# Agent attention and a gated convolution: three of five shifted operand rows copied by VectorE instead of by DMA

## The chip, the cores and the metric

The kernel runs on one core of a Trainium2 chip. The time is what the device takes for one execution, in microseconds (us). Before the change the median of three runs is 430.09 us (429.39 to 432.08). The core has TensorE (PE in the profile, with PEld for its weight loads), VectorE (DVE), ScalarE (ACT), GpSimd (POOL), and SyncE (SP), whose queue issues nearly all DMAs of this kernel; 16 DMA engines move the data.

## The reference

The inputs are q, k and v of 4 batches, 12800 rows and 128 channels, 49 "agent" rows per batch, and three weight arrays. Agents attend to the keys; the queries attend to the agents; the result passes a causal convolution of 5 taps per channel as a sigmoid gate, beside a linear projection, and a second projection.

```python
a2k = sm(agents, k)             # softmax(scale * agents @ k^T): 49 x 12800
agent_v = a2k @ v               # 49 x 128
q2a = sm(q, agents)             # 12800 x 49
x = q2a @ agent_v               # 12800 x 128
gate_pre = sum(conv_w[k] * shifted(x, 4 - k) for k in range(5))
out = (sigmoid(gate_pre) * (x @ w_val)) @ w_out
```

## The kernel before

Rows run along the free dimension. The kernel never forms x. What the gate and the value need is linear in the 49 query weights q2a, so per batch the convolution's taps, `w_val` and `agent_v` are folded into small weight tiles (`fold_weights`, line 110): tile `stat` holds eight 128x128 f16 blocks, five for the taps, one for the value, and two "rest" blocks that carry what f16 rounding leaves.

**Query weights as matmul operand.** A unit is 1280 rows, 10 units to a batch, 40 in all. For a unit (`queries`, line 667) TensorE makes scores, VectorE transposes them in 32x32 blocks, takes the maximum, and with GpSimd (subtract) and ScalarE (exp) forms the softmax `qw`. Tile `pt` then gets, per row, 128 f16 columns: 49 rounded weights (ScalarE, line 713), 49 rounding rests (GpSimd, line 726), and the first 30 rounded weights once more (GpSimd, line 718), so that they can meet the rest of the weights' own rounding. `transposes` (line 734) turns `pt` into 1280 columns of `x1`: for units 0 to 3 by TensorE with two copies (ScalarE line 764, VectorE line 769), for the other 36 by a DMA transpose that SP issues (line 743).

**The second operand x2.** The other 19 agents do not fit into the 128 rows of `x1`. `shifts` (line 774) copies rows 29 to 48 of `x1` (20 rows; `X2LO`, `X2R`) to five places of `x2`, one for each tap, each shifted by one more column, by five DMAs (line 791): once for each of the units 0 to 3 and then once for each pair of units, 18 pairs. `x2` has three buffers of 2560 columns.

**Chunks.** The output is made in chunks of 512 rows, 100 of them, the last in two halves. For a chunk TensorE runs five gate matmuls (line 828), one with `x2` (line 832), one for the value (line 855) and one with `x2` for it (line 859). ScalarE makes tanh `th` (line 841), VectorE the product `h` (line 868), ScalarE its f16 part `hh` (line 874), GpSimd the rest `hl` (line 879). Two chunks later TensorE projects with three matmuls (lines 898 to 900), ScalarE scales into `ob` (line 912) and SP stores it. The gate and the value have one PSUM bank each: TensorE can start the value of the next chunk only when `h` has read this one's.

**Order.** Every step is entered in a `Plan` with its engine, a cost in us and what it reads and writes. TensorE's steps keep the order in which they are entered (a list that weaves scores, agent values, the fold and the chunks together). The other engines' and SP's steps are put in order by a list scheduler (`Plan.order`, line 89) that goes by the entered costs and the length of the chain behind a step; a DMA is taken to land after its bytes and 1.4 us (`LAND`), and no more than 8 are in flight (`LANES`). What comes out is a fixed order on each engine; at run time each engine takes its instructions strictly in that order and waits where an operand is late.

Of the kernel before, what the change touches and what calls it, by code (L numbers as in the profile page):

```python
# [9 lines left out]
F32 = mybir.dt.float32  # L10
# [4 lines left out]
AX = mybir.AxisListType  # L15
# [16 lines left out]
X2LO = 29  # L32
X2R = 20
# [18 lines left out]
T_AT = 7  # L52
HOP = 0.09
# [9 lines left out]
class Plan:  # L63
# [7 lines left out]
    def __init__(self):  # L71
        self.steps, self.urge = [], []
        self.wrote, self.read = {}, {}

    def add(self, engine, us, fn, reads=(), writes=(), moved=0.0, key=None, urge=0.0):
# [11 lines left out]
        self.urge.append(urge)  # L87

    def order(self):
# [32 lines left out]
        while done < n:  # L122
# [49 lines left out]
def tile_agent_attention_gated_conv(  # L172
# [11 lines left out]
    A = 49  # L184
    NU = N // UNIT
# [12 lines left out]
    def ring(n, shape, dtype, name, pool=const):  # L198
        return [pool.tile(shape, dtype, name=f"{name}{i}") for i in range(n)]
# [12 lines left out]
    qw = ring(3, [P, NBLK, A], F32, "qw")  # L212
# [52 lines left out]
    for t in wst_sb:  # L265
        nc.gpsimd.memset(t[:, TAPS + 1 :, :], 0.0)

# [6 lines left out]
    def weights():  # L274
# [4 lines left out]
        else:  # L279
# [51 lines left out]
            for fn in ops:  # L331
# [5 lines left out]
                out=cmax, in_=conv_sb, axis=AX.X, op=ALU.max, apply_absolute_value=True  # L337
# [41 lines left out]
    def key_scores(b, u):  # L379
# [13 lines left out]
        if not first:  # L393
# [5 lines left out]
                out=kmx[b % 2][:, u, :], in_=src, axis=AX.X, op=ALU.max  # L399
# [6 lines left out]
    def key_max(b):  # L406
# [6 lines left out]
                out=m2, in_=kmx[x].rearrange("p u j -> p j u"), axis=AX.X, op=ALU.max  # L413
# [9 lines left out]
        def spread():  # L423
            nc.vector.tensor_reduce(
                out=mrow, in_=p1[0:2, 0:P].rearrange("j (g a) -> j a g", g=G),
                axis=AX.X, op=ALU.max,
# [58 lines left out]
    def fold_weights(b):  # L485
# [19 lines left out]
        def normalise():  # L505
            dve.tensor_scalar_add(den, pt[:, 0:A], 1e-9)
            dve.reciprocal(out=den, in_=den)
            dve.tensor_tensor(out=avT, in0=pt[:, AP_ : AP_ + A], in1=den, op=ALU.mult)

# [10 lines left out]
        def gate_scale():  # L520
            dve.tensor_reduce(
                out=mx[:, 0:1], in_=avT, axis=AX.X, op=ALU.max, apply_absolute_value=True
# [18 lines left out]
        x2g = wst[:, TAPS + 1, 0 : TAPS * X2R].rearrange("p (k r) -> p k r", k=TAPS)  # L541
        x2v = wst[:, TAPS + 2, 0 : TAPS * X2R].rearrange("p (k r) -> p k r", k=TAPS)
        ghi = wst[:, 0:TAPS, 0:A]
        vhi = wst[:, TAPS, 0:A]
        off = NDUP - X2LO

# [6 lines left out]
        def val_weights():  # L553
            dve.tensor_reduce(
                out=mx[:, 1:2], in_=pv[:, 0:A], axis=AX.X, op=ALU.max,
# [8 lines left out]
            rest(wst[:, TAPS, 2 * A :], pv[:, 0:NDUP], 1, vhi[:, 0:NDUP])  # L564
            rest(x2v[:, HALO, off:], pv[:, NDUP:A], 1, vhi[:, NDUP:])
# [10 lines left out]
        add("dve", 1.2, val_weights, [at_v], [(*w_, "v"), "mxv"])  # L576
        add(
            "act", 0.4,
            lambda: nc.scalar.copy(out=wst[:, 0:TAPS, A : 2 * A], in_=ghi),
# [3 lines left out]
            "act", 0.22, lambda: nc.scalar.copy(out=wst[:, TAPS, A : 2 * A], in_=vhi),  # L583
            [(*w_, "v")], [(*w_, "e")],
        )
        add("dve", 0.7, gate_rest, ["gw", (*w_, "g")], [(*w_, "r")])
# [46 lines left out]
        def split():  # L633
            dve.tensor_reduce(
                out=oscale, in_=po[:, 0:P], axis=AX.X, op=ALU.max, apply_absolute_value=True
# [31 lines left out]
    def queries(b, u):  # L667
# [6 lines left out]
        sa = sT[:, :, 0:A]  # L674
# [4 lines left out]
            lambda: nc.vector.tensor_reduce(out=qmx[x], in_=sa, axis=AX.X, op=ALU.max),  # L679
# [5 lines left out]
                out=d, in0=sa, in1=qmx[x].unsqueeze(2).to_broadcast([P, NBLK, A]),  # L685
# [10 lines left out]
        def sums():  # L696
            nc.vector.tensor_reduce(out=sm, in_=e, axis=AX.X, op=ALU.add)
# [9 lines left out]
                out=w, in0=e, in1=r.unsqueeze(2).to_broadcast([P, NBLK, A]), op=ALU.mult  # L707
# [5 lines left out]
            "act", 0.58, lambda: nc.scalar.copy(out=pt[:, :, 0:A], in_=w),  # L713
# [5 lines left out]
                out=pt[:, :, 2 * A :], in0=w[:, :, 0:NDUP], scalar1=1.0, scalar2=0.0,  # L719
# [7 lines left out]
                out=pt[:, :, A : 2 * A], in0=w, in1=pt[:, :, 0:A], op=ALU.subtract  # L727
# [7 lines left out]
    def transposes(b, u):  # L735
# [3 lines left out]
        if not on_pe(b, u):  # L739
# [7 lines left out]
                [(*p_, n) for n in range(3)], [("x1", u)], 2.4,  # L747
# [26 lines left out]
    def shifts(b, u):  # L774
# [9 lines left out]
        src = [(x, v) for v in range(max(u0 - 1, 0), u + 1) for x in ("x1", "x1b")]  # L784
        for k in range(TAPS):
            c = PAD - HALO + u0 * UNIT + k

            q, e = (nc.scalar, "act") if g == 0 and k % 2 else (nc.sync, "dma")
            add(
                e, 0.75,  # L790
                lambda k=k, c=c, q=q: q.dma_start(
                    out=x2[k * X2R : (k + 1) * X2R, o : o + n * UNIT],
                    in_=x1[X2LO : X2LO + X2R, c : c + n * UNIT],
                ),
                src, [("x2", s % 3, o + i * UNIT, k) for i in range(n)], 0.26 * n,
            )
# [6 lines left out]
    def gates(t):  # L803
# [17 lines left out]
        x2k = [("x2", segs_[0] % 3, h, k) for h in halves for k in range(TAPS)]  # L821
# [3 lines left out]
        def matmuls():  # L825
            for k in range(TAPS):
# [6 lines left out]
                out=pg, lhsT=stat[0 : TAPS * X2R, TAPS + 1, :],  # L833
                rhs=x2[0 : TAPS * X2R, o2 : o2 + w], start=False, stop=True,
# [13 lines left out]
    def values(t):  # L848
# [5 lines left out]
        def matmuls():  # L854
# [5 lines left out]
                out=pv, lhsT=stat[0 : TAPS * X2R, TAPS + 2, :],  # L860
                rhs=x2[0 : TAPS * X2R, o2 : o2 + w], start=False, stop=True,
# [196 lines left out]
```

## Time and profile before

| | |
|---|---|
| median of 3 runs | 430.09 us |
| the profiled execution's own time | 431.22 us |
| its span in the profile | 429.4 us |
| mean granted TensorE clock | 0.996 |
| busy: PE, DVE, ACT, POOL | 402.9, 297.0, 300.4, 224.3 us |
| DMA: bytes moved, mean rate | 128.07 MB, 298 GB/s |

The span is the time from the first to the last instruction, and 1.8 us of the execution's time lie outside of it. In the rows that follow, "x5" is a count of instructions; in a row of waits stand the total, the number and the longest; in a timeline stand start, length, engine, line, and in brackets the idle time of the engine just before, with what ended it.

### The profile page before, as it was taken

Reading aid. Unit: us, or ns where it says so; the run is one execution under the profiler, and the core shown is the slowest. Engines: PE = TensorE matmul, PEld = TensorE weight load, DVE = VectorE, ACT = ScalarE, POOL = GpSimd, SP = SyncE. Lnnn points to the kernel's source line nnn. Section 1 sums busy time; section 2 is a strip of 40 time slices with the busy share of each in tenths; the row PEclk is TensorE's granted clock in tenths of the full one; section 3 lists DMA queues with packets and bytes.
Section 4 is the critical chain, followed back from the end, with each engine's and each line's share of the span. In section 5 each row is a group of like instructions: output and inputs, shape, how many; then the busy total and the mean of one; then the engine's idle time right before and its main releaser. Section 6 shows DMA issues by size and latency. Waiting matters only on the chain.

```text
span 429.4 us, 8968 instructions
## 1 busy us (share of the span) xinstructions
PE 402.9 (94%) x3307; PEld 194.8 (45%) x3307; DVE 297.0 (69%) x555; ACT 300.4 (70%) x520; POOL 224.3 (52%) x239
## 2 busy tenths in 40 slices
PE   3978888999999999999999999999999999999995
PEld 1357333345565444444555544445555544434443
DVE  3776879886786877578666887678666787566231
ACT  1464536678976577778876676778876577777875
POOL 1002246564466665544557665553356466687553
PEclk9999989999999999999999999999999999999999
DMA  8999999999999999999999999999999999887743
GB/s 288 422 415 415 371 350 337 297 285 309 343 358 294 249 270 289 307 309 305 340 329 356 292 323 292 320 312 334 306 330 257 289 291 287 215 199 173 192 156 122
DMA packets 76158, 128.07 MB, mean 298 GB/s; under 512 B 51644, under 2 KB 51900, under 8 KB 76116
## 3 DMA queue, kind: packets, MB, share of 16 engines
q1 hardware_dynamic: 76056, 127.41, 96.0%
q8 instruction: 26, 0.43, 0.4%
q14 instruction: 16, 0.13, 0.1%
q10 hardware_dynamic: 60, 0.10, 0.1%
HBM read 79.25 MB, written 26.21 MB: 246 GB/s over the span
## 4 chain that ended last, share of the span: by engine, by line
PE 65%; DMA 13%; DVE 12%; ACT 5%; issue 3%; SPq 1%; POOL 1%; DVEq 0%; ACTq 0%; POOLq 0%
PE gate L828 20%; PE sc L363 13%; PE av L463 6%; PE gate L832 4%; PE val L855 4%; PE val L859 4%; PE out L898 4%; PE out L899 4%; PE out L900 4%; DMA ld<-qT 3%; DMA ld<-vP 3%; DVE h L868 2%; ACT e L455 2%; DMA ld<-kT 2%; DMA outT<-ob 2%
## 5 line engine op out<-in xcount | busy, mean ns | idle before, releaser
L879 POOL TENSOR_TENSOR hl<-h,hh 128x512 f16<-128x512 f32 (+1 forms) x101 | 117.0, 1160 | 121.3 <-ACT hh L874 113.7
L828 PE MATMUL gate<-x,stat 128*128 128x512 f16 (+1 forms) x500 | 124.4, 378 | 2.4 <-ACT th L841 2.3
L868 DVE SCALAR_TENSOR_TENSOR h<-th,val 128x512 f32<-128x512 f32 x100 | 67.7, 677 | 69.1 <-PE out L899 46.1
L363 PE MATMUL sc<-ld,ag_sb 128*32 128x320 f32 x1280 | 102.0, 452 | 10.0 <-DMA ld<-kT 8.0
L912 ACT ACTIVATE ob<-out,oscale 128x512 f32<-128x512 f32 x98 | 67.2, 686 | 23.5 <-PE out L900 17.4
L841 ACT ACTIVATE th<-gate,unscale 128x512 f32<-128x512 f32 x100 | 68.3, 683 | 19.7 <-PE gate L832 18.0
L828 PEld LDWEIGHTS <-stat 128*128 128x128 f16 x505 | 45.6, 97 | 66.4 <-issue 19.0
L874 ACT CAST hh<-h 128x512 f16<-128x512 f32 (+1 forms) x101 | 61.4, 608 | 13.1 <-DVE h L868 12.4
L684 POOL TENSOR_TENSOR qw<-sT,qmx 128x490 f32<-128x490 f32 x40 | 41.5, 1038 | 50.2 <-DVE qmx L679 50.1
L363 PEld LDWEIGHTS sc<-ld,ag_sb 128*32 128x32 f32 x1280 | 37.0, 112 | 62.8 <-issue 22.5
L463 PE MATMUL av<-ld,eT 128*64 128x129 f32 x800 | 49.5, 275 | 1.7 <-DMA ld<-vP 1.4
L389 ACT COPY ks<-sc 128x640 f32<-128x640 f32 x40 | 27.7, 691 | 32.7 <-PE sc L363 30.6
L463 PEld LDWEIGHTS av<-ld,eT 128*64 128x64 f32 x800 | 43.7, 136 | 11.7 <-issue 7.3
L726 POOL TENSOR_TENSOR pt<-qw,pt 128x490 f16<-128x490 f32 x40 | 44.7, 1119 | 3.8 <-ACT pt L713 3.1
L455 ACT ACTIVATE e<-ks,kbias 128x320 f32<-128x320 f32 x80 | 39.0, 553 | 6.1 <-DVE kbias L444 3.3
L373 DVE STREAM_TRANSPOSE eT<-e 128x640 f32<-128x640 f32 x40 | 33.6, 842 | 11.4 <-ACT e L455 5.9
L373 DVE STREAM_TRANSPOSE sT<-sc 128x640 f32<-128x640 f32 x40 | 33.3, 834 | 10.8 <-PE sc L363 10.6
L398 DVE TENSOR_REDUCE kmx<-ks 128x2 f32<-128x640 f32 x39 | 31.4, 817 | 11.8 <-ACT ks L389 11.8
L832 PE MATMUL gate<-x,stat 100*128 100x512 f16 x100 | 38.0, 380 | 0.8 <-DMA x<-x 0.8
L855 PE MATMUL val<-x,stat 128*128 128x512 f16 x100 | 37.8, 378 | 0.1
L859 PE MATMUL val<-x,stat 100*128 100x512 f16 x100 | 37.8, 378 | 0.0
L898 PE MATMUL out<-hh,wo 128*128 128x512 f16 x98 | 37.1, 379 | 0.0
(125 smaller groups left out, 392.1 us busy)
## 6 DMA issues: line engine op xcount, KB each, us to landing
ld<-vP SPq DMA_DIRECT2D x40, 645.0 KB
ld<-kT SPq DMA_DIRECT2D x40, 640.0 KB
ld<-qT SPq DMA_DIRECT2D x40, 640.0 KB
outT<-ob SPq DMA_DIRECT2D x48, 512.0 KB
x<-x SPq DMA_DIRECT2D x90, 100.0 KB
x<-x SPq DMA_DIRECT2D x18, 50.0 KB
outT<-ob SPq DMA_DIRECT2D x3, 256.0 KB
x<-pt SPq DMA_TRANSPOSE x36
```

The costliest lines, as they stand in the source:

```text
L363: nc.tensor.matmul(out=out[g * BLK : (g + 1) * BLK, j, 0:GT], lhsT=ag_sb[:, b, j * BLK : (j + 1) * BLK], rhs=src[:, g * GT : (g + 1) * GT] ...
L373: nc.vector.transpose(out=out.rearrange("p n (j i) -> p j n i", j=2), in_=in_.rearrange("p j (n i) -> p j n i", i=BLK),)
L463: nc.tensor.matmul(out=av[o : o + AP_, 0 : C + 1], lhsT=et[:, n, :], rhs=vt[:, n, :], start=(u == 0 and n < 2), stop=(u == NU - 1 and n >= ...
L828: nc.tensor.matmul(out=pg, lhsT=stat[:, k, :], rhs=x1[:, c : c + w], start=(k == 0), stop=False,)
L832: nc.tensor.matmul(out=pg, lhsT=stat[0 : TAPS * X2R, TAPS + 1, :], rhs=x2[0 : TAPS * X2R, o2 : o2 + w], start=False, stop=True,)
L841: lambda: nc.scalar.activation(out=th, in_=pg, func=AF.Tanh, scale=unscale[:, 0:1]),
L855: nc.tensor.matmul(out=pv, lhsT=stat[:, TAPS, :], rhs=x1[:, PAD + n0 : PAD + n0 + w], start=True, stop=False,)
L859: nc.tensor.matmul(out=pv, lhsT=stat[0 : TAPS * X2R, TAPS + 2, :], rhs=x2[0 : TAPS * X2R, o2 : o2 + w], start=False, stop=True,)
L868: lambda: nc.vector.scalar_tensor_tensor(out=h, in0=th, scalar=1.0, in1=pv, op0=ALU.add, op1=ALU.mult),
L874: "act", 0.16 + 0.42 * scale, lambda: nc.scalar.copy(out=hh, in_=h),
L879: lambda: nc.gpsimd.tensor_tensor(out=hl, in0=h, in1=hh, op=ALU.subtract),
L912: lambda: nc.scalar.activation(out=ob[:, o : o + w], in_=po, func=AF.Copy, scale=oscale),
```

## The change

**Rows of x1.** The rows of `x1` (the columns of `pt`) now begin with two agents in duplicate: rows 0 and 1 are agents 28 and 29 once more, rows 2 to 50 the 49 rounded weights, 51 to 99 the rests, 100 to 127 agents 0 to 27 again. The host puts the two extra agents ahead of the others in the agents' array, so scores, subtraction, exp and product run over 51 columns instead of 49; the sum leaves the two out, and the duplicate copy of line 718 is 28 columns wide instead of 30. By this the 19 agents that go to `x2` stand in rows 32 to 50, the beginning of a quarter of the 128 partitions.

**x2.** Its 128 rows are now used as five blocks by tap: taps 0, 2 and 4 at rows 0, 32 and 64, tap 1 at row 97, tap 3 in two pieces at rows 116 and 20. Taps 0, 2 and 4 are copied by VectorE (19 rows, 1280 or 2560 columns), taps 1 and 3 by three DMAs of 20, 12 and 8 rows; of an odd number of rows one more is moved, which meets a weight of zero. The two matmuls with `x2` read 128 rows instead of 100, and GpSimd zeroes the three `x2` buffers once at the start. In the fold the rest weights now go to more places: nine short VectorE instructions instead of four. The planner is told that a DMA transpose lands 2 us later than before for those who wait for it (`SPARE`).

```diff
+A0 = 2
+HI0, LO0, DUP0 = A0, 51, 100
+REST = 32
+X2_ROWS = (
+    ((0, 19, 0),),
+    ((0, 19, 97),),
+    ((0, 19, 32),),
+    ((0, 12, 116), (12, 7, 20)),
+    ((0, 19, 64),),
+)
+SPARE = 2
...
-                end = max(wire, when + us) + LAND
-                lanes = lanes[1:] + [end]
+                end = max(wire, when + us) + LAND + self.spare[i]
+                lanes = lanes[1:] + [end - self.spare[i]]
...
+    for t in x2s:
+        nc.gpsimd.memset(t, 0.0)
...
-            rest(wst[:, TAPS, 2 * A :], pv[:, 0:NDUP], 1, vhi[:, 0:NDUP])
-            rest(x2v[:, HALO, off:], pv[:, NDUP:A], 1, vhi[:, NDUP:])
+            rest(wst[:, TAPS, DUP0:], pv[:, 0 : P - DUP0], 1, vhi[:, 0 : P - DUP0])
+            rest(wst[:, TAPS, 0:A0], pv[:, P - DUP0 : NDUP], 1, vhi[:, P - DUP0 : NDUP])
+            for i, n, r in X2_ROWS[HALO]:
+                i += NDUP
+                rest(wst[:, TAPS + 2, r : r + n], pv[:, i : i + n], 1, vhi[:, i : i + n])
...
-            rest(wst[:, 0:TAPS, 2 * A :], gw[:, :, 0:NDUP], 0, ghi[:, :, 0:NDUP])
-            rest(x2g[:, :, off:], gw[:, :, NDUP:], 0, ghi[:, :, NDUP:])
+            n = P - DUP0
+            rest(wst[:, 0:TAPS, DUP0:], gw[:, :, 0:n], 0, ghi[:, :, 0:n])
+            rest(wst[:, 0:TAPS, 0:A0], gw[:, :, n:NDUP], 0, ghi[:, :, n:NDUP])
+            quads = wst[:, TAPS + 1, 0 : 3 * REST].rearrange("p (k r) -> p k r", k=3)
+            rest(quads[:, :, 0:NREST], gw[:, 0:TAPS:2, NDUP:], 0, ghi[:, 0:TAPS:2, NDUP:])
+            for k in range(1, TAPS, 2):
+                for i, n, r in X2_ROWS[k]:
+                    i += NDUP
+                    rest(
+                        wst[:, TAPS + 1, r : r + n], gw[:, k, i : i + n], 0,
+                        ghi[:, k, i : i + n],
+                    )
...
         for k in range(TAPS):
             c = PAD - HALO + u0 * UNIT + k
...
-            add(
-                e, 0.75,
-                lambda k=k, c=c, q=q: q.dma_start(
-                    out=x2[k * X2R : (k + 1) * X2R, o : o + n * UNIT],
-                    in_=x1[X2LO : X2LO + X2R, c : c + n * UNIT],
-                ),
-                src, [("x2", s % 3, o + i * UNIT, k) for i in range(n)], 0.26 * n,
-            )
+            for i, m, r in X2_ROWS[k]:
+                out, in_ = x2[r : r + m, o : o + w], x1[REST + i : REST + i + m, c : c + w]
+                keys = [("x2", s % 3, o + j * UNIT, k, i) for j in range(n)]
+                if k % 2 == 0:
+                    add(
+                        "dve", 0.08 + 0.33 * n,
+                        lambda out=out, in_=in_: nc.vector.tensor_copy(out=out, in_=in_),
+                        src, keys,
+                    )
+                    continue
...
+                add(
+                    e, 0.75, lambda out=out, in_=in_, q=q: q.dma_start(out=out, in_=in_),
+                    src, keys, 0.013 * m * n,
+                )
...
-                out=pg, lhsT=stat[0 : TAPS * X2R, TAPS + 1, :],
-                rhs=x2[0 : TAPS * X2R, o2 : o2 + w], start=False, stop=True,
+                out=pg, lhsT=stat[:, TAPS + 1, :], rhs=x2[:, o2 : o2 + w],
+                start=False, stop=True,
```

TensorE's order stays as it was. On the other engines much is moved; three places follow. The first is VectorE in the fold of the first batch, between the rounded value weights and `unscale`; `wst0` is the tile of folded weights, `val` and `gw` what they are made of, `rs` their scale. Before:

```order
L548 SCALAR_TENSOR_TENSOR wst0_118<-val_131,rs_162,wst0_118 128x30
L548 SCALAR_TENSOR_TENSOR wst0_118<-val_131,rs_162,wst0_118 128x19
L548 SCALAR_TENSOR_TENSOR wst0_118<-gw_161,rs_162,wst0_118 128x5x30
L548 SCALAR_TENSOR_TENSOR wst0_118<-gw_161,rs_162,wst0_118 128x5x19
L613 TENSOR_SCALAR unscale0_124<-mx_160 128x2
```

The same place now:

```order
L561 SCALAR_TENSOR_TENSOR wst0_118<-val_131,rs_165,wst0_118 128x28
L561 SCALAR_TENSOR_TENSOR wst0_118<-val_131,rs_165,wst0_118 128x2
L561 SCALAR_TENSOR_TENSOR wst0_118<-val_131,rs_165,wst0_118 128x19
L561 SCALAR_TENSOR_TENSOR wst0_118<-gw_164,rs_165,wst0_118 128x5x28
L561 SCALAR_TENSOR_TENSOR wst0_118<-gw_164,rs_165,wst0_118 128x5x2
L561 SCALAR_TENSOR_TENSOR wst0_118<-gw_164,rs_165,wst0_118 128x3x19
L561 SCALAR_TENSOR_TENSOR wst0_118<-gw_164,rs_165,wst0_118 128x19
L561 SCALAR_TENSOR_TENSOR wst0_118<-gw_164,rs_165,wst0_118 128x12
L561 SCALAR_TENSOR_TENSOR wst0_118<-gw_164,rs_165,wst0_118 128x7
L639 TENSOR_SCALAR unscale0_124<-mx_163 128x2
```

Four instructions became nine over the same 294 elements per partition; nothing else moved between them.

The second place is VectorE in the third batch, around the product `h0` of chunk 60 (chunks are counted from 0); `eT` and `sT` are block transposes of key and query scores, `qmx` a maximum. Before:

```order
L868 SCALAR_TENSOR_TENSOR h2_108<-th2_105,val_131 128x512
L373 STREAM_TRANSPOSE sT1_86<-sc0_128 128x2x10x32
L679 TENSOR_REDUCE qmx1_88<-sT1_86 128x10
L373 STREAM_TRANSPOSE eT2_84<-e0_80 128x2x10x32
L373 STREAM_TRANSPOSE eT0_82<-e1_81 128x2x10x32
L373 STREAM_TRANSPOSE eT1_83<-e0_80 128x2x10x32
L868 SCALAR_TENSOR_TENSOR h0_106<-th0_103,val_131 128x512
```

The same place now, where `x21` is the buffer of `x2` for units 26 and 27:

```order
L910 SCALAR_TENSOR_TENSOR h2_108<-th2_105,val_131 128x512
L389 STREAM_TRANSPOSE sT1_86<-sc0_128 128x2x10x32
L821 COPY x21_101<-x1_99 19x2560
L389 STREAM_TRANSPOSE eT2_84<-e0_80 128x2x10x32
L389 STREAM_TRANSPOSE eT0_82<-e1_81 128x2x10x32
L910 SCALAR_TENSOR_TENSOR h0_106<-th0_103,val_131 128x512
L821 COPY x21_101<-x1_99 19x2560 x2
L910 SCALAR_TENSOR_TENSOR h1_107<-th1_104,val_131 128x512
```

One copy now stands ahead of two transposes and the `h` of chunk 60, and two more ahead of the `h` of chunk 61; the maximum `qmx1` and one transpose went behind.

The third place is SP for the same pair of units: `pt0` is unit 27, whose transpose completes the pair. Before:

```order
L927 DMA outT<-ob1_116 128x1024
L743 DMA_TRANSPOSE x1_99<-pt0_96 128x10x128
L358 DMA ld6_67<-qT 128x1280
L358 DMA ld7_68<-vP 128x1290
L358 DMA ld8_69<-vP 128x1290
L791 DMA x21_101<-x1_99 20x2560 x5
L927 DMA outT<-ob2_117 128x1024
```

The same place now:

```order
L770 DMA_TRANSPOSE x1_99<-pt0_96 128x10x128
L969 DMA outT<-ob1_116 128x1024
L374 DMA ld0_61<-vP 128x1290
L969 DMA outT<-ob2_117 128x1024
L833 DMA x21_101<-x1_99 20x2560
L833 DMA x21_101<-x1_99 12x2560
L833 DMA x21_101<-x1_99 8x2560
```

Five DMAs of 20 rows became three of 20, 12 and 8, an output now stands behind the transpose instead of ahead of it, and the load of slot 0, which stood later, is ahead of the three.

More of the change, by code (lines that the diff above doesn't have):

```diff
@@ L820, in gates @@
         xs = [("x1", u) for u in units] + [("x1b", u) for u in units]
[L821 removed]
+        x2k = [
+            ("x2", segs_[0] % 3, h, k, i) for h in halves for k in range(TAPS)
+            for i, _, _ in X2_ROWS[k]
+        ]
         st = [("stat", x, 0), ("stat", x, 1)]
```

80 lines of the change are left out of this document (43 added, 37 removed).

## The prediction

> **What bounds the kernel now.** I read the page first, then the busy times by stretch, then TensorE's waits, and last the timelines of VectorE, GpSimd and SP around one pair of units.
>
> ```profile
> span 429.4 us, 8968 instructions
> PE 402.9 (94%) x3307; PEld 194.8 (45%) x3307; DVE 297.0 (69%) x555; ACT 300.4 (70%) x520; POOL 224.3 (52%) x239
> PE   3978888999999999999999999999999999999995
> DMA  8999999999999999999999999999999999887743
> ```
>
> ```profile
> 38.00:90.00 52.00, 46.05 (x456) 21.32 (x460) 43.45 (x88) 28.96 (x49) 24.53 (x29) 0.97 1.00 343
> 390.00:430.00 40.00, 34.83 (x168) 15.97 (x166) 12.16 (x19) 29.77 (x51) 20.59 (x20) 0.99 0.49 157
> ```
>
> ```profile
> 90.00:390.00 300.00, 295.56 (x2355) 142.63 (x2348) 217.64 (x401) 222.85 (x389) 175.25 (x180) 1.00 1.02 298
> ```
>
> Columns are the stretch, its length, and busy time of PE, PEld, DVE, ACT and POOL, then the granted clock, the DMA engines' share and GB/s. TensorE is the bound: from 90 to 390 us it stands still for 4.4 us (300 less 295.56), from 38 to 90 for 6.0, in the last stretch for 5.2, where the last output leaves. Its instructions are not changed. So the change cannot win more than some 10 us, and only by ending waits of TensorE; what it can lose has no such end. VectorE has 27% left in the long stretch, but only 16% from 38 to 90 (43.45 of 52). The DMA engines have nothing left until 370 us. TensorE's waits are these:
>
> ```profile
> PE sc L363 <- DMA ld<-kT: 8.0, 4, 7.1
> PE gate L828 <- ACT th L841: 2.3, 6, 0.7
> PE val L655 <- DVE wsp L642: 1.9, 1, 1.9
> PE sc L363 <- DVE sT L373: 1.9, 3, 0.8
> PE sc L757 <- POOL pt L726: 1.2, 1, 1.2
> PE gate L593 <- DVE wst L548: 1.1, 1, 1.1
> PE gate L832 <- DMA x<-x: 0.8, 1, 0.8
> ```
>
> Of all of them one, 0.8 us, is for the DMAs into `x2` that the change takes up. Five name VectorE, or what waits for it, and VectorE gets work.
>
> **The change part by part.** *What SP and the DMA engines lose.* The rows of the shifts, and their sizes:
>
> ```profile
> L791 SPq DMA_DIRECT2D x<-x x108: 706/713/2455, 41.2 to 406.4; - x108
> ```
>
> ```profile
> x<-x SPq DMA_DIRECT2D x90, 100.0 KB
> x<-x SPq DMA_DIRECT2D x18, 50.0 KB
> ```
>
> A pair costs SP three issues instead of five, so 2 x 0.71 = 1.4 us less, and 200 KB instead of 500 KB are moved (40 rows of 100). Over 18 pairs that is 5.4 MB of 128. It ends the wait of 0.8 us: **-0.8**. The rest is hidden as long as TensorE does not wait for SP.
>
> *What VectorE gets.* No row shows a copy from SBUF to SBUF of 16-bit elements; these lie nearest:
>
> ```profile
> L769 DVE COPY x<-sc 128x640 f16<-128x640 f16 x4 | 2.0, 492 | 2.5 <-ACT x L764 2.5
> L291 DVE TENSOR_SCALAR ob<-ob 128x261 int32<-128x261 int32 x6 | 1.7, 295 | 3.4 <-DMA ob<-moe 3.3
> L613 DVE TENSOR_SCALAR unscale<-mx 128x2 f32<-128x2 f32 x4 | 0.6, 159 | 0.0
> ```
>
> L291 less L613 is 136 ns for 259 words of 4 bytes, 0.53 ns a word, beside 0.16 us that any instruction costs. The copy L769, out of PSUM, takes 0.52 ns an element (492 less 159, over 640). A copy of 2560 elements therefore takes 0.16 + 1280 x 0.53 ns = 0.83 us if it goes by words, 0.16 + 2560 x 0.52 ns = 1.49 us if by elements; one of 1280 takes 0.50 or 0.83. I take words, since L291 is the row with both ends in SBUF. 54 copies x 0.83 and 12 x 0.50 make 51 us (by elements 90), and VectorE's 297 become 348, 81% of the span. From 90 to 390 it has 15 pairs, 45 x 0.83 = 37 us, so 255 of 300, 85%. That lies beside TensorE's work except where a copy stands right ahead of an `h`. By the Trainium skill, VectorE: DVE Perf Modes, the tier table, a 16-bit copy within SBUF runs at four elements a cycle; the estimate from its 693 ns for 2048 elements is near the word reading, and under it the slow reading would have no chance; no run here shows it yet.
>
> *Copies ahead of h.* How little an `h` can be late shows at chunk 60 (DVE, then PE):
>
> ```profile
> 299.84 1.75 DVE L373 STREAM_TRANSPOSE eT<-e 128x640 f32<-128x640 f32 x2 [0.22 <-ACT e L455]
> 301.77 0.84 DVE L373 STREAM_TRANSPOSE eT<-e 128x640 f32<-128x640 f32 x1 [0.18 <-ACT e L455]
> 302.54 0.65 DVE L868 SCALAR_TENSOR_TENSOR h<-th,val 128x512 f32<-128x512 f32 x1
> ```
>
> ```profile
> 303.66 0.38 PE L855 MATMUL val<-x,stat 128*128 128x512 f16 x1
> ```
>
> It ends at 303.19 and the next value begins at 303.66: 0.47 us. In the new order a copy stands right ahead of an `h` for 16 of the 18 pairs. The planner means them for time in which VectorE would wait anyway; what it does not know is how long one can be held up. The rows of VectorE's instructions with two inputs in SBUF show such holding up:
>
> ```profile
> L698 DVE SCALAR_TENSOR_TENSOR qsm<-qsm,tiny x40: 170/171/974, 34.4 to 392.7; 128x10 f32<-128x10 f32 x40
> L698 DVE SCALAR_TENSOR_TENSOR qsm<-qsm,tiny 128x10 f32<-128x10 f32 x40 | 12.2, 305 | 1.4
> ```
>
> The median is 171 ns, the longest 974, the mean 305: 0.13 us on average for the same ten elements. If copies are held up like it, 16 x 0.13 = 2.1 us, of which the 0.47 us of room takes about half: **+1.0**, between 0 (all within the room) and 16 x 0.8 = 13 (all as the longest). The Trainium skill (SBUF — State Buffer, Who interferes with whom) has a lock for this: a VectorE instruction in a two-port mode, which a copy within SBUF can be, and a GpSimd instruction shut each other out for a whole instruction; without that rule for copies this term would be 0 and the sum 1.0 lower.
>
> *The fold.* TensorE waits 1.1 us for it in the first batch:
>
> ```profile
> 46.61 0.39 DVE L548 SCALAR_TENSOR_TENSOR wst<-val,rs,wst 128x30 f16<-128x30 f32 x2
> 46.92 0.60 DVE L548 SCALAR_TENSOR_TENSOR wst<-gw,rs,wst 128x150 f16<-128x150 f32 x2
> 47.43 0.17 DVE L613 TENSOR_SCALAR unscale<-mx 128x2 f32<-128x2 f32 x1
> ```
>
> Two instructions over 49 elements took 0.31 us from start to start, two over 245 took 0.51; so an element costs 1.0 ns and an instruction 0.13 us beside. Five more over the same elements are 5 x 0.13 = 0.65 us, all on the path: **+0.7**. The three later folds have the same 0.65 each amid chunks; TensorE has other work there, and I count half: **+1.0** (0 to 2.0).
>
> *At one price.* Zeroing `x2` costs GpSimd at most 3 x 10 x 0.31 = 9.3 us, by the first row below, and is hidden in the 28 us ahead of its first subtraction, by the second:
>
> ```profile
> L266 POOL MEMSET wst<- x2: 311/311/311, 1.8 to 2.0; 128x256 f16 x2
> 30.80 1.02 POOL L684 TENSOR_TENSOR qw<-sT,qmx 128x490 f32<-128x490 f32 x1 [28.48 <-DVE qmx L679]
> ```
>
> Without that cover it would be up to 9 us. 51 columns for 49 lengthen that subtraction by 4%, 0.04 us a unit; GpSimd has idle time, so 0 (all 40 units: 1.7). 128 rows for 100 in the two matmuls cost nothing: 378 and 380 ns stand for both heights in the rows of the groups.
>
> ```profile
> L832 PE MATMUL gate<-x,stat 100*128 100x512 f16 x100 | 38.0, 380 | 0.8 <-DMA x<-x 0.8
> L855 PE MATMUL val<-x,stat 128*128 128x512 f16 x100 | 37.8, 378 | 0.1
> ```
>
> *The wait that moves.* The copies read what a DMA transpose wrote. Till now SP waited for it, with loads and outputs behind; now VectorE does too, with transposes and `h` behind, and TensorE behind those. How late it is can be read at units 7 and 27 (last rests on GpSimd, then SP's transpose and shifts):
>
> ```profile
> 89.71 2.15 POOL L726 TENSOR_TENSOR pt<-qw,pt 128x490 f16<-128x490 f32 x2
> 285.71 1.10 POOL L726 TENSOR_TENSOR pt<-qw,pt 128x490 f16<-128x490 f32 x1 [0.18 <-ACT pt L713]
> ```
>
> ```profile
> 95.76 2.39 SPq L743 DMA_TRANSPOSE x<-pt  x1
> 299.38 4.17 SPq L743 DMA_TRANSPOSE x<-pt  x1
> 306.63 3.80 SPq L791 DMA_DIRECT2D x<-x  x5
> ```
>
> Unit 7 was ready at 91.86 and issued at 95.76, 3.9 us later; unit 27 was ready at 286.81 and issued at 299.38, 12.6 later, and had landed by 306.63. SP falls behind by (12.6 - 3.9) / 10 = 0.87 us a pair. The new order puts a copy of this pair ahead of the rows at 299.84. That would be 6.8 us too early, if SP were as late as now. But SP saves 1.4 us a pair, more than the 0.87 it loses; its lag should stay near 3.9 us, and the transpose land 8.7 us earlier, at 298, in time. So **0** here; the other end is a rival.
>
> *The sum.* -0.8 + 1.0 + 0.7 + 1.0 = +1.9 us on the profiled execution's 431.22 (429.4 of span, 1.8 outside). The median of the runs is 1.1 lower, so 430.09 + 1.9 = **432.0 us**, within 1% (4.3 us), which is about what a measurement here can tell from no change. Its own range is 429 (all costs hidden) to 436 (copies held up by 0.3 us each time).
>
> **The rivals.** *Late transposes (slower).* SP and the DMA engines stay behind, because it is the transposes themselves that take long (1.35 to 8.09 us to issue, in the row below) while the DMA engines are full, and 4% of the bytes less changes little.
>
> ```profile
> L743 SPq DMA_TRANSPOSE x<-pt x36: 1346/2810/8086, 76.4 to 399.8; - x36
> SPq L791 <- DMA x<-pt: 26.1, 15, 3.9
> ```
>
> Then VectorE takes over waits such as the second row's. Say half of the 8.7 us is gained: the transpose of unit 27 lands at 302.3, the copy takes 0.83, the transposes of 299.84 their 1.75, and `h` begins at 304.9 instead of 302.54, 2.4 late, 1.9 past its room. With four such pairs in the second and third batch, where the lag is largest, that is 8 us: **440 us**. It decides from a landing at 300.4 on (303.66 less 0.65, 1.75 and 0.83). For it: planner positions are fixed, and any of 18 pairs can be late. Against it: the arithmetic of the lag.
>
> *Slow copies (slower).* By elements the copies take 45 x 1.49 = 67 us of the 300, VectorE is at 285 of 300, 95%, with any holding up on top; the 30 us more find about half of their room: **447 us**.
>
> *Waits go (faster).* With SP and the DMA engines freed, transposes and loads come earlier, and the planner's new order ends the waits for `pt`, `th`, `sT` and `wsp` too: two thirds of 8.1 us (2.3 + 1.9 + 1.9 + 1.2 + 0.8), less 0.7 for the fold, is -4.7: **425 us**. Against it: all of these but 0.8 us wait for VectorE and its followers.
>
> **How the numbers follow.** Forecast 0.42, late transposes 0.34, slow copies 0.06, waits go 0.18. Faster by over 1%: 0.17 of the last. Slower: both slower rivals and the forecast's upper end, 0.42. Within 1%: 0.41. The range runs from 425, the faster rival, to 441, just past the late transposes; it leaves out the slow copies and the far halves of two rivals.
>
> **What would show it.** Right: copies of 0.7 to 0.9 us; VectorE at about 348 us; the first wait for `wst` at 1.8 us; no wait of VectorE's copies for `x<-pt` over 1 us; SP's lag at unit 27 under 6 us. Wrong: copies that wait for transposes ahead of an `h`, with TensorE's waits for `h` or `th` grown (late transposes); copies of 1.5 us; or fewer waits from 38 to 90 us (faster).

## The result and the profile after

The changed kernel takes **448.24 us** (median, 447.19 to 449.13). The kernel before took 431.08 us beside it, and the ratio is 1.0397, with a 95% interval from 1.0343 to 1.0452: 17 us slower. The profiled execution took 447.19 us. The forecast was 432.0 us, and the range ended at 441. Slower had the largest chance (0.42), but 0.40 of it came from late transposes and slow copies, and neither happened, as shown below. So the sign was given its chance by luck, and no case had the size by the mechanism that acted.

The head of the page of the changed kernel, with the rows of TensorE and the DMA engines by slices:

```profile
span 445.3 us, 8992 instructions
PE 405.2 (91%) x3307; PEld 194.8 (44%) x3307; DVE 365.9 (82%) x641; ACT 302.4 (68%) x520; POOL 243.7 (55%) x242
PE   4888789899979898999999999999999999989995
DVE  5877989888998899798788899897879898798451
DMA  8999999887989999999989999999979724444633
```

TensorE's own work grew by 2.3 us only (402.9 to 405.2), and the time of the span in which it stood still by 13.6 (429.4 less 402.9 is 26.5, 445.3 less 405.2 is 40.1). VectorE went from 297 to 366 us, where 348 was forecast. GpSimd went from 224 to 244 us, where next to nothing but the zeroing was forecast. The busy times by stretch, in the columns of the prediction's rows, say where this was lost:

```profile
38.00:90.00 52.00, 44.44 (x456) 20.57 (x455) 45.66 (x96) 27.59 (x46) 23.97 (x26) 1.00 0.97 357
90.00:390.00 300.00, 285.83 (x2296) 138.01 (x2289) 260.15 (x453) 217.12 (x377) 177.83 (x172) 1.00 0.91 270
```

From 90 to 390 us TensorE stands still for 14.2 us (300 less 285.83), where it was 4.4. VectorE is busy for 87% of that stretch. The DMA engines' share fell from 1.02 to 0.91, but not evenly, as two parts of the stretch show:

```profile
90.00:345.00 255.00, 242.67 (x2003) 118.62 (x1996) 221.76 (x376) 186.27 (x325) 149.12 (x143) 1.00 0.98 295
345.00:390.00 45.00, 43.16 (x295) 19.39 (x293) 38.39 (x78) 30.84 (x53) 28.71 (x30) 1.00 0.46 130
```

Up to 345 us they are still full (0.98, before 1.03); what was gained is that their work ends sooner, so that the next 45 us are at 0.46 (before 0.95). The time was lost elsewhere: 12.3 of the 14.2 us in which TensorE stands still lie ahead of 345 us. TensorE's waits of the changed kernel name the place:

```profile
PE sc L379 <- DMA ld<-kT: 7.7, 5, 6.6
PE sc L379 <- DVE sT L389: 7.0, 7, 1.5
PE val L897 <- DVE h L910: 4.9, 10, 0.9
PE gate L870 <- ACT th L883: 3.3, 5, 1.1
PE gate L874 <- DVE x L821: 2.0, 2, 1.4
PE val L681 <- DVE wsp L668: 1.9, 1, 1.9
PE sc L784 <- POOL pt L752: 1.8, 2, 1.1
PE gate L619 <- DVE wst L561: 1.4, 1, 1.4
```

Line 389 is VectorE's block transpose (373 before), 910 is `h`, 821 the new copy. The waits for `sT` grew by 5.1 us (1.9 to 7.0), those of the value matmul for `h` from nothing to 4.9, those for the copies themselves from nothing to 2.0, those for `th` by 1.0 and those for `pt` by 0.6. Together that is 13.6 us. The wait of 0.8 us for the shift DMAs is gone, the fold's grew by 0.3. Nearly all of the growth is VectorE being late, or those who follow it (`th`'s bank, `pt`).

Why VectorE is late stands in the rows of the copies. First the instructions of line 821 (shortest, median and longest in ns), then their group with its busy time and mean:

```profile
L821 DVE COPY x<-x x66: 480/818/1800, 41.1 to 426.2; 19x2560 f16<-19x2560 f16 x54, 19x1280 f16<-19x1280 f16 x12
```

```profile
L821 DVE COPY x<-x 19x2560 f16<-19x2560 f16 (+1 forms) x66 | 64.4, 975 | 1.7
```

The median copy of 2560 elements took 0.82 us, the shortest of 1280 elements 0.48. At these two durations the 66 copies would take 54 x 0.82 + 12 x 0.48 = 50.0 us; they took 64.4. So 14.4 us, 0.22 us a copy on average, are time in which a copy was held up, up to 1 us for a single one. It is not spread evenly: 28 of the 66 took over 0.05 us longer than the shortest of their size, and every one of the 28 overlaps an instruction of GpSimd in the trace, where of the other 38 only 16 do. How this goes is to be seen where three copies stand in a row. Timelines of VectorE and GpSimd around 121 to 125 us (start, length):

```profile
120.72 1.00 DVE L821 COPY x<-x 19x2560 f16<-19x2560 f16 x1
121.73 1.69 DVE L821 COPY x<-x 19x2560 f16<-19x2560 f16 x1
123.45 1.60 DVE L821 COPY x<-x 19x2560 f16<-19x2560 f16 x1
```

```profile
119.51 1.54 POOL L752 TENSOR_TENSOR pt<-qw,pt 128x490 f16<-128x490 f32 x1
121.42 1.32 POOL L921 TENSOR_TENSOR hl<-h,hh 128x512 f16<-128x512 f32 x1 [0.38 <-ACT hh L916]
122.70 1.67 POOL L752 TENSOR_TENSOR pt<-qw,pt 128x490 f16<-128x490 f32 x1
```

The ends alternate: GpSimd at 121.05, copy at 121.72, GpSimd at 122.74, copy at 123.42, GpSimd at 124.37, copy at 125.05. Each copy ends 0.67 to 0.68 us after the GpSimd instruction ahead of it, and each of the two later GpSimd instructions 1.02 and 0.95 us after the copy ahead of it, a little less than they take undisturbed (0.82 us for the copy, 1.16 and 1.09 for the others, in rows below). They take turns, a whole instruction at a time. TensorE paid for this one:

```profile
125.10 0.38 PE L874 MATMUL gate<-x,stat 128*128 128x512 f16 x1 [1.41 <-DVE x L821]
```

The Trainium skill (SBUF — State Buffer, Who interferes with whom) says that a VectorE copy in a two-port mode and GpSimd's instructions lock each other out of a shared pair of ports for a whole instruction; these rows agree with it.

GpSimd pays as well. The subtraction `hl` (line 879 before, 921 now) had a mean of 1160 ns before, and has 1213 now, 5.4 us over 101 of them. Before, then now:

```profile
L879 POOL TENSOR_TENSOR hl<-h,hh 128x512 f16<-128x512 f32 (+1 forms) x101 | 117.0, 1160 | 121.3 <-ACT hh L874 113.7
L921 POOL TENSOR_TENSOR hl<-h,hh 128x512 f16<-128x512 f32 (+1 forms) x101 | 122.4, 1213 | 118.2 <-ACT hh L916 118.0
```

The rival with the largest chance, late transposes, did not happen. No copy waited for a transpose: the profile has no idle time of VectorE ahead of line 821 that ends with one. Unit 27's rests (GpSimd) and SP's transpose now read:

```profile
300.59 1.09 POOL L752 TENSOR_TENSOR pt<-qw,pt 128x490 f16<-128x490 f32 x1 [0.22 <-ACT pt L739]
```

```profile
301.71 2.88 SPq L770 DMA_TRANSPOSE x<-pt  x1
```

The rests end at 301.68, the transpose is issued at 301.71: SP has no lag left, where it had 12.6 us. The rests themselves come 14.9 us later than before (286.81), as VectorE's work ahead of them does, and so the transpose still comes 2.3 us later than before (299.38). In the run with short copies below, which takes no longer than the kernel before, the rests end at 290.34 and the transpose is issued at 290.37: there the lag is gone as well.

### The profile page after: what moved, and what is told of

It reads as the page before. It is cut to its first block, busy times and chain, and to the rows that moved or that the text cites. A ratio compares the mean times of both kernels' runs of the same rounds, so it can differ in the third digit from the quotient of the medians.

```text
span 445.3 us, 8992 instructions
## 1 busy us (share of the span) xinstructions
PE 405.2 (91%) x3307; PEld 194.8 (44%) x3307; DVE 365.9 (82%) x641; ACT 302.4 (68%) x520; POOL 243.7 (55%) x242
## 4 chain that ended last, share of the span: by engine, by line
PE 54%; DVE 23%; DMA 8%; ACT 6%; issue 5%; POOL 2%; SPq 1%; DVEq 0%; ACTq 0%; POOLq 0%
PE gate L870 16%; PE sc L379 10%; PE av L479 6%; DVE x L821 6%; DVE h L910 6%; PE val L897 4%; PE out L941 3%; PE out L940 3%; PE val L901 3%; PE gate L874 3%; DMA ld<-qT 3%; PE out L942 3%; DMA ld<-vP 3%; ACT th L883 2%; DVE qsm L723 2%
## 5 line engine op out<-in xcount | busy, mean ns | idle before, releaser
L921 POOL TENSOR_TENSOR hl<-h,hh 128x512 f16<-128x512 f32 (+1 forms) x101 | 122.4, 1213 | 118.2 <-ACT hh L916 118.0
L821 DVE COPY x<-x 19x2560 f16<-19x2560 f16 (+1 forms) x66 | 64.4, 975 | 1.7
L710 POOL TENSOR_TENSOR qw<-sT,qmx 128x510 f32<-128x510 f32 x40 | 43.8, 1098 | 36.7 <-DVE qmx L705 36.5
L752 POOL TENSOR_TENSOR pt<-qw,pt 128x490 f16<-128x490 f32 x40 | 47.2, 1182 | 3.8 <-ACT pt L739 3.5
L897 PE MATMUL val<-x,stat 128*128 128x512 f16 x100 | 37.7, 377 | 5.2 <-DVE h L910 4.9
L874 PE MATMUL gate<-x,stat 128*128 128x512 f16 x100 | 37.8, 378 | 2.0 <-DVE x L821 2.0
L732 DVE TENSOR_TENSOR qw<-qw,qr 128x510 f32<-128x510 f32 x40 | 38.3, 958 | 0.5
L901 PE MATMUL val<-x,stat 128*128 128x512 f16 x100 | 37.8, 378 | 0.0
```

The source lines that it names most:

```text
L821: lambda out=out, in_=in_: nc.vector.tensor_copy(out=out, in_=in_),
L874: nc.tensor.matmul(out=pg, lhsT=stat[:, TAPS + 1, :], rhs=x2[:, o2 : o2 + w], start=False, stop=True,)
L897: nc.tensor.matmul(out=pv, lhsT=stat[:, TAPS, :], rhs=x1[:, PAD + n0 : PAD + n0 + w], start=True, stop=False,)
L901: nc.tensor.matmul(out=pv, lhsT=stat[:, TAPS + 2, :], rhs=x2[:, o2 : o2 + w], start=False, stop=True,)
L921: lambda: nc.gpsimd.tensor_tensor(out=hl, in0=h, in1=hh, op=ALU.subtract),
```

## The experiments

The theory after these readings: VectorE and GpSimd hold each other up over the copies (**holding up**), and this makes most of the 17 us. The first rival: the copies' plain time on VectorE, 50 us on an engine that has other work with deadlines (**load**). Further rivals: the new order and the waits in it, the new layout with its longer fold, and the plan's wrong prices.

**Copies of 16 columns.** The order, waits, layout, fold and zeroing of the changed kernel, but each copy moves 16 columns only; the rest of what the three taps read stays out of the result. The order is that of the changed kernel on every engine.

```diff
-lambda out=out, in_=in_: nc.vector.tensor_copy(out=out, in_=in_),
+lambda out=out, in_=in_: nc.vector.tensor_copy(out=out[:, 0:16], in_=in_[:, 0:16]),
```

> The changed kernel with every copy cut to its first 16 columns, so most of x2's rows for taps 0, 2 and 4 stay zero and the output leaves that part out; order, waits and all else stay as they are. Load and lock theory: copies of 0.2 us, 431 to 435 us. If it is the waits of copies on late DMA transposes, or the new order itself: 442 or more.

Measured: **430.27 us**, ratio 0.9987 [0.9961, 1.0013]. The copies of this kernel (shortest, median, longest in ns):

```profile
L821 DVE COPY x<-x x66: 159/162/1100, 41.0 to 408.2; 19x16 f16<-19x16 f16 x66
```

All of the 17 us hang on the length of the copies; the order, the fold, the 51 columns, the 128 rows and what the freed DMAs bring come to nothing together. The run says two things more. These copies are held up too: they take 18.9 us in all, where 66 at the median would take 10.7, and the 8.2 us between cost nothing that can be measured. So held-up time is not lost time by itself. Whether it is free here because VectorE has more room (321.2 us busy, where the changed kernel has 365.9) or because such short copies do not hold GpSimd up in turn (`hl` has a mean of 1158 ns), this run does not tell. And even so the change gains nothing: the DMA engines that it relieves were full, but TensorE waited only 0.8 us for the DMAs that it takes away, and of the 8.0 us for key loads 7.1 are one wait at the very start.

**The same time on VectorE, with another instruction.** Each copy is replaced by a max-reduce over 640 or 320 of the columns, which takes as long on VectorE (808 and 476 ns) and writes two columns; the copied taps are left out. The order is again that of the changed kernel on every engine.

```diff
-lambda out=out, in_=in_: nc.vector.tensor_copy(out=out, in_=in_),
+lambda out=out, in_=in_, n=n: nc.vector.tensor_reduce(
+    out=out[:, 0:2], in_=in_[:, 0 : 320 * n].rearrange("p (j i) -> p j i", j=2),
+    axis=AXIS, op=ALU.max),
```

> The changed kernel with each copy put in by a maximum over 640 (or 320) elements of the same x1 rows, at the same place in the order: by the 0.81 us of the key maxima it takes VectorE as long as a copy of 2560 (0.82), but the 39 key maxima show no spread that would come from GpSimd. The output leaves out x2's share for taps 0, 2 and 4. Load theory: 444 to 449 us, as the changed kernel. Lock theory: 432 to 437 us, with GpSimd's hl back from 1213 to about 1160 ns.

Measured: **433.90 us**, ratio 1.0081 [1.0053, 1.0109]. The busy times, the reduces, and `hl` in this kernel:

```profile
PE 402.0 (93%) x3307; PEld 194.5 (45%) x3307; DVE 351.7 (81%) x641; ACT 302.6 (70%) x520; POOL 231.1 (53%) x242
```

```profile
L821 DVE TENSOR_REDUCE x<-x x66: 474/808/812, 40.9 to 412.8; 19x2 f16<-19x640 f16 x54, 19x2 f16<-19x320 f16 x12
L821 DVE TENSOR_REDUCE x<-x 19x2 f16<-19x640 f16 (+1 forms) x66 | 49.4, 748 | 1.6
L925 POOL TENSOR_TENSOR hl<-h,hh 128x512 f16<-128x512 f32 (+1 forms) x101 | 116.9, 1159 | 118.4 <-ACT hh L920 118.1
```

No reduce took over 812 ns, though 44 of the 66 overlap an instruction of GpSimd. With the same order and 49.4 us of reduces on VectorE the kernel loses 3.6 us against the short copies (433.9 less 430.3), and the changed kernel 14.3 more (448.2 less 433.9). Against this run its VectorE is 14.2 us longer (365.9 less 351.7) and its GpSimd 12.6 (243.7 less 231.1). `hl` is back at 1159 ns, and TensorE's waits for `sT` and for `h` in the value matmul are back near their size:

```profile
PE sc L379 <- DVE sT L389: 3.6, 6, 1.5
PE val L901 <- DVE h L914: 1.3, 4, 0.4
```

The same section of the Trainium skill says that on this chip VectorE's reduces never contend with GpSimd; the run agrees. So load is 3.6 us, and holding up, on an engine that carries this load, 14.3 us more, as far as copy and reduce differ in nothing else that matters (a reduce writes two columns, a copy all). The next runs take the other side of the pair away.

**Less work on GpSimd beside the copies.** `hl` is cut from 512 columns to 16, the rest stays zero (the second half of `h`'s precision is left out). GpSimd's busy time falls from 243.7 to 147.4 us; VectorE's list stays, but for three zeroings of `hl` at the start.

```diff
-lambda: nc.gpsimd.tensor_tensor(out=hl, in0=h, in1=hh, op=ALU.subtract),
+lambda: nc.gpsimd.tensor_tensor(
+    out=hl[:, 0:16], in0=h[:, 0:16], in1=hh[:, 0:16], op=ALU.subtract),
```

> The changed kernel with GpSimd's subtraction hl cut from 512 columns to 16 (the rest of hl stays zero, so the second half of h's precision is left out of the values); some 100 us of GpSimd's work are gone, VectorE's list is the same. If copies and GpSimd's instructions hold each other up: copies near 0.85 us on average instead of 0.975, and 432 to 438 us. If VectorE's load alone is the cause: copies as before at 0.975 and 445 us or more.

Measured: **433.35 us**, ratio 1.0058 [1.0026, 1.0091]. The copies of this kernel:

```profile
L823 DVE COPY x<-x 19x2560 f16<-19x2560 f16 (+1 forms) x66 | 55.4, 839 | 1.9 <-issue 0.2
```

They lost 9.0 of their 14.4 us of being held up (64.4 to 55.4), though the copies and their order are the same, and the time fell by 14.9 us. The 12 copies that are still over 0.05 us longer than the shortest all overlap an instruction of GpSimd, in 11 of them one that makes `pt` or `qw`.

**The controls.** The same cut in the kernel before, and in the kernel with reduces in place of copies.

> The control for the run before it: the kernel before, with the same cut of hl to 16 columns. If GpSimd's hl matters only through the copies that it holds up: the same as the kernel before, 429 to 432 us. If hl is a cost of its own: a gain of several us here too, and the gain of the changed kernel from the cut has to be read net of it.

> The fourth cell beside three runs (copies with full hl, the max-reduces of equal length in place of the copies with full hl, copies with hl cut to 16 columns): max-reduces in place of the copies and hl cut to 16 columns, so three of the five taps and the second half of h's precision are left out. If the loss is copies and GpSimd's work holding each other up: the cut brings little once the copies are gone, 430 to 434 us beside 433.9 us with the full hl. If the cut helps by itself whatever VectorE runs: it brings as much as in the changed kernel, down to 420 us.

Measured: 430.58 us, ratio 0.9973 [0.9935, 1.0011], for the kernel before; **428.58 us**, ratio 0.9943 [0.9921, 0.9966], with reduces. Side by side:

| on VectorE | `hl` of 512 columns | `hl` of 16 | what the cut brings |
|---|---|---|---|
| copies | 448.24 | 433.35 | 14.9 us |
| max-reduces of the same length | 433.90 | 428.58 | 5.3 us |
| kernel before | 430.86 | 430.58 | nothing measurable |

The cut brings 5.3 us beside the reduces too, more than was expected: a shorter `hl` is worth something without any copy. VectorE's busy time falls by 11.6 us with it (351.7 to 340.1), and nearly all of that is the product `qw`, an instruction with two inputs in SBUF, like those that the prediction's row of line 698 showed held up. With the full `hl`, then with the short one:

```profile
L732 DVE TENSOR_TENSOR qw<-qw,qr 128x510 f32<-128x510 f32 x40 | 38.4, 961 | 0.5
L734 DVE TENSOR_TENSOR qw<-qw,qr 128x510 f32<-128x510 f32 x40 | 27.6, 693 | 0.5
```

How much of the 5.3 us comes by this, and how much by an earlier `hl`, is open. The 9.6 us beyond (14.9 less 5.3; the intervals of the four runs leave it uncertain by some 3 us) belong to copies and `hl` meeting. Read the other way, the copies cost 14.3 us over the reduces with the full `hl` and 4.8 with the short one.

**The right prices in the plan.** The planner held a copy for 0.41 or 0.74 us (0.08 + 0.33 a unit). Here it is told 0.68 and 1.08, near what they took on average.

```diff
-"dve", 0.08 + 0.33 * n,
+"dve", 0.28 + 0.40 * n,
```

> The changed kernel, with the planner's price of a copy raised from 0.08 + 0.33 us a part to 0.28 + 0.40 us a part, which is what the copies measured (1.08 for two parts, 0.68 for one). If the loss comes from a plan that holds the copies for too short: 440 us or less. If it comes from the holding up itself, wherever the copies stand: 445 to 450 us.

Measured: 449.33 us, ratio 1.0403 [1.0366, 1.0439]; the order is another one, the time is not. The copies were held up a little more:

```profile
L821 DVE COPY x<-x 19x2560 f16<-19x2560 f16 (+1 forms) x66 | 70.5, 1068 | 2.0 <-DMA x<-pt 0.2
```

So the plan's wrong price is not the cause. That a plan which knows the average does not know when GpSimd will be in the way would explain it; no run shows that.

**No copy, one, two.** The taps go back to DMA one by one, in the new layout, with the plan made anew each time. In the first two runs the first segment's DMAs for taps above 1 were all issued from ScalarE's queue.

```diff
-if k % 2 == 0:
+if k in DVE_TAPS:      # (), (0,) or (0, 4)
```

> The new layout of x1 and x2, its nine fold instructions, 51 columns and zeroing stay; all five taps go by DMA (six DMAs a pair, 20, 20, 20, 20, 12 and 8 rows) and VectorE copies nothing. Load theory (the time that the copies take on VectorE's fixed order is the loss) and lock theory (the holding up between copies and GpSimd is the loss) both expect 431 to 434 us. If the other edits were the loss: 440 or more.

> As the first of these kernels, but tap 0 is copied by VectorE (18 copies of 2560 and 4 of 1280, some 17 us of VectorE) and taps 1 to 4 go by DMA; the planner orders anew. Load theory: the loss grows faster than the load, so one copy in three costs little, 431 to 436 us. Lock theory: each copy costs its share, a third of the loss, 436 to 439 us.

Measured: 449.37 us without a copy (1.0458 [1.0407, 1.051]) and 437.54 with one (1.0157 [1.012, 1.0195]). Neither can be read as meant, since the edit also gave ScalarE's queue four issues in a row. ScalarE of the kernel without copies, from 40 us on:

```profile
41.12 9.08 ACTq L834 DMA_DIRECT2D x<-x  x4
50.25 0.63 ACT L719 ACTIVATE qw<-qw 128x510 f32<-128x510 f32 x1 [9.69 <-DMA x<-x]
```

Four issues held ScalarE's queue for 9.1 us, the exponential of line 719 behind them, and TensorE's fold waited 5.7 us for VectorE behind that. In the next three runs only tap 3's two pieces are issued there, as in the changed kernel.

```diff
-q, e = (nc.scalar, "act") if g == 0 and k > 1 else (nc.sync, "dma")
+q, e = (nc.scalar, "act") if g == 0 and k == 3 else (nc.sync, "dma")
```

> All five taps go by DMA in the new layout, two of them in three pieces: six shift DMAs a pair, no copy on VectorE. The first pair's issues on ACT's queue are cut to the two pieces of tap 3, as in the changed kernel, so that ACT is not held for 9 us ahead of the first fold. If the copies on VectorE (their load and their being held up) are the whole cost: near the kernel before, 429 to 434 us, GpSimd's subtraction of hl at 1.16 us, first wait for qsm near nothing. If the layout itself (128 rows, six DMAs of which the pieces end at odd partitions) costs: 440 us or more, with TensorE's waits for the DMA x<-x as in the run before (6 us).

> Only tap 0 is copied by VectorE, four taps by DMA, and ACT's queue issues only the two pieces of tap 3 for the first pair. If the cost goes with the number of copies (17 us for three a pair): 6 us over the kernel with none, 435 to 438 us. If one copy fits into VectorE's idle time and it is the crowding near full load that costs: within 2 us of the kernel with none, 430 to 433 us.

> Taps 0 and 4 are copied by VectorE, three taps by DMA. By the number of copies: 11 us over the kernel with none, 440 to 443 us. By crowding alone: much nearer to the kernel with one copy than to that with three, 433 to 437 us.

| copies a pair | us | ratio and interval |
|---|---|---|
| none | 443.57 | 1.0297 [1.0270, 1.0323] |
| one | 434.48 | 1.0084 [1.0069, 1.0099] |
| two | 441.63 | 1.0261 [1.0238, 1.0284] |
| three (the change) | 448.24 | 1.0397 [1.0343, 1.0452] |

From one copy to three each costs some 7 us (7.2 and 6.6), net of the DMA that it saves, as so much for each copy would have it; crowding alone does not fit, since the second costs as much as the third. The support is weak, though: each kernel has an order of its own, the kernel with one copy is in neither range that was expected, and by the sum used above the copies were held up 1.0, 9.8 and 14.4 us, which is not so much each. And "none" was expected near the kernel before, and is 13 us over it. Putting the copies back to DMAs does not undo the change: in the new layout an all-DMA pair has six shift DMAs, not five. TensorE's waits there, two rows:

```profile
PE gate L875 <- DMA x<-x: 6.1, 4, 2.0
PE gate L871 <- ACT th L884: 5.1, 8, 1.4
```

**The sixth DMA alone.** The kernel before, tap 1 of each pair cut into two DMAs of 12 and 8 rows: the same bytes, one issue more.

```diff
+cut = (0, 12, X2R) if k == 1 and g else (0, X2R)
+for i, j in zip(cut, cut[1:]):    # rows i to j of tap k
```

> The kernel before, old layout, with tap 1 of each pair cut into two DMAs (12 and 8 rows): six shift DMAs a pair instead of five, the same bytes, no copy on VectorE. The kernel with all taps by DMA in the new layout has six too and took 443.57 us. If the sixth issue on SP is what cost it 13 us (SP is the queue that was late): 437 to 444 us here. If it is something of the new layout: 430 to 433 us.

Measured: **437.27 us**, ratio 1.0123 [1.0093, 1.0153], at the lower end of what was expected of the sixth issue. One more issue of 0.7 us for each pair and each single unit but the first (21 x 0.7 = 15 us of SP's time), and the plan made with it, cost 6 us in the old layout. If they cost as much in the new one, that is 6 of the 13; where the other 7 us of "none" come from wasn't found. No version of these computes the reference faster than the kernel before.

## Why the prediction was wrong

**The step that failed is the term "copies ahead of h", +1.0 us.** The mechanism was named, a lock between copies and GpSimd; the size was off by a factor of more than ten (1.0 forecast, 17.9 measured, load included). Three choices in it were wrong.

1. *Which instructions count.* The term counted 16 copies, one for each pair that has one right ahead of an `h`; the other 50 were left out, as the planner "means them for time in which VectorE would wait anyway". But VectorE takes its list in order: what any copy loses moves everything behind it, and on an engine at 87% of the stretch little of it is caught up before the next deadline. TensorE's waits show the loss at `sT` first (5.1 us), not only at `h` (4.9).
2. *By which row a copy was priced.* 0.13 us was the mean loss of a VectorE instruction of 0.17 us. A copy of 0.82 us meets more of GpSimd's instructions, and can have to wait for a whole one: measured 0.22 us each, up to 1.0. The upper bound of 13 us took 0.8 us as the longest wait, which was near (1.0 measured), but again for 16 copies.
3. *Who pays.* A lock has two sides. The term had none for GpSimd, whose instructions became 12.6 us longer beside copies than beside reduces, and so `hl` and `pt` later.

Measured in the place of +1.0: 3.6 us of load and 14.3 of holding up on top of it, by the run with reduces. Held-up time has no fixed price: 8.2 us of it on VectorE cost nothing measurable in the run with short copies.

The other steps, one by one:

- **-0.8, the shift DMAs:** right in that the wait went, and SP's lag with it. But no gain shows: the run with short copies is at the time of the kernel before (-1.7 to +0.6 us by its interval), and TensorE has one wait of 1.7 us there for the DMAs into `x2` that are left.
- **Copies by words, 0.83 and 0.50 us:** right; 0.82 and 0.48 where undisturbed, so the trace agrees with the tier table of the Trainium skill (VectorE: DVE Perf Modes) that the prediction set beside it. The rival of slow copies (1.49 us) fell. Its 447 us stands near the result by accident: VectorE went past the 348 us of the forecast to 366 mostly by being held up (14.4 us), not by copying slowly.
- **The fold, +0.7:** its length was right. The same stretch of VectorE, from the first `wst` to `unscale`, took 46.61 to 47.43 us before; it now takes 46.67 to 48.13, 0.64 us more for five instructions, as these rows of the changed kernel show:

```profile
46.67 0.52 DVE L561 SCALAR_TENSOR_TENSOR wst<-val,rs,wst 128x28 f16<-128x28 f32 x3
47.11 1.11 DVE L561 SCALAR_TENSOR_TENSOR wst<-gw,rs,wst 128x140 f16<-128x140 f32 x6
48.13 0.16 DVE L639 TENSOR_SCALAR unscale<-mx 128x2 f32<-128x2 f32 x1
```

  TensorE's wait grew by 0.3 us only (1.1 to 1.4, not to 1.8), and in the run with short copies all terms but that of the copies, forecast at +0.9 together, came to -0.6 us (-1.7 to +0.6). No run has the fold alone.
- **Zeroing, 51 columns, 128 rows, at nothing:** nothing speaks against it in that same run, which has them only together with the rest. The zeroing took 6.6 us of GpSimd, and 9.3 had been the bound.
- **The wait that moves, 0:** right, and with it the rival of late transposes (0.34) fell, since SP's lag went to zero (3.9 us had been expected to stay). The kernel with one copy, where SP still issues five, shows what it would have looked like: its copies waited 4.2 us in three places for `x<-pt`.
- **"Waits go":** the chance of 0.18 was too high. Four of the five waits named there have VectorE or its followers in them, as the prediction itself held against it; and the run with short copies gained nothing.

Slower (0.42) was ahead of same (0.41) by a hair, and through rivals that did not happen: that was luck. The profile bore more. VectorE at 81%, and copies that may have to take turns with a GpSimd at 52%, were reason enough to multiply the held-up time by all copies: 66 x 0.13 = 8.6 us, from the row that the prediction quoted, in the place of 1.0, which makes 439.6 us the centre, without any room taken off. Even that is half of the loss.

## What to carry to other kernels

Before work is moved from a full engine to one with idle time, ask how long the bound engine waits for what is to be moved: here it was 0.8 us, so next to nothing could be won, whatever the share of busy time said. When the receiving engine shares a resource with another, price each moved instruction by its own length and the other's instruction length, for all of them and on both engines, and ask how much room the receiving engine has left to make up for it; a substitute instruction of equal length that doesn't use the resource separates load from contention in one run. And a layout that came with the change has its own price when the change is taken back: check "undo one part" against the kernel before, not against zero.

## What the runs showed of the hardware that was not expected

- Copies of 19 x 2560 16-bit elements on VectorE and GpSimd's subtractions of 128 x 490 and 128 x 512 took turns strictly, five times in a row from 121.05 to 125.05 us. Over all copies this made 14.4 us on 50.
- The product `qw` on VectorE, with two inputs in SBUF, had a mean of 961 ns beside `hl` of 512 columns and 693 ns beside `hl` of 16, with reduces in the place of the copies in both kernels.
- A copy from partition 32 on to partitions 0 or 64 took no longer than one within its partitions: in the kernel with one copy, which goes from 32 to 0, the median is 816 ns, in the changed kernel, where a third of them stay at 32, 818.
- One more DMA issue a pair, the bytes being the same, cost 6 us of 431 (ratio 1.0123), with the order made anew and the DMA engines as full as they are here. Four issues on ScalarE's queue at 41 us held it for 9.08 us, 2.3 us each; two at the same place in the changed kernel took 2.05 us, and those of SP take 0.71 each in the median.
